# A written-out order, a rearranged start, and additions by GpSimd's DMAs in a two-layer attention and MLP kernel

## The chip, the cores and the metric

The kernel runs on one core of a Trainium2 chip. The core has TensorE (PE, matmuls; its weight loads are shown as PEld), VectorE (DVE), ScalarE (ACT), GpSimd (POOL) and SyncE (SP), each with its own in-order instruction stream, and 16 DMA engines. DMAs are issued here from SP's queue, four from ScalarE's, and after the change also from GpSimd's. The metric is the device time of one execution in microseconds (us).

## The reference

Input is `x`, 2048 tokens of 640 float32 values. Two layers, each an attention block and an MLP block, use the same weights:

```python
x = x + _A_ref(_layernorm(x, axis=-1), A_wqkv, A_wo)
x = x + _B_ref(_layernorm(x, axis=-1), B_w1, B_b1, B_w2, B_b2)
```

The attention has 32 heads of 20 values. Each token attends to 8 tokens: itself and those 2, 4, ... 14 places before it. The MLP has 1536 hidden values, a GELU and two biases.

## The kernel before, in words

**Units.** Because the window steps by 2, even and odd tokens never meet. Each parity is cut in two, which makes four units of 512 tokens per layer, n = 0 to 3 for the first layer and n = 4 to 7 for the second. A unit has four token tiles t of 128 partitions x 640 values. Attention works in four head groups g.

**Precision.** Matmuls are float16 with each operand split in a high and a low part: high x high, low x high and high x low are added in PSUM. So a product over 640 has 5 blocks x 3 passes = 15 matmuls. Weights are scaled by 64 (`WS`) before they are split, and results by 1/64.

**A unit's path.** Layernorm (`layernorm`); transposes of the normed high and low parts (for unit 0 on TensorE through `turn`, L498 to L506, and for all others by DMA transposes from SP, L623); the q, k, v product (`qkv`, L657, 480 columns per group and tile; ScalarE evicts it, L663); a spill to DRAM and a fetch back with neighbours; attention on VectorE (`attention`, L731 to L769: long multiplies and reductions, 2.8 to 5.5 us each); transposes by DMA (L789); the projection (`project`, two halves c of 320 columns per tile, L800); its addition to the token stream (L806, on VectorE, straight from PSUM); a second layernorm (its power of -1/2 is a small GpSimd instruction, L593; the normed tile is ScalarE's L613, its float16 cast L616); and the MLP (`mlp`, L837 to L879, and for the last three units `mlp_fast`, L1014 to L1133, a scheme with seven products instead of eight). The MLP's second bias `b2` is added to the token stream after the second layernorm has read it: by a GpSimd instruction (L627) in units 0 to 6, by VectorE in unit 7.

**Buffers.** The product and projection results share three PSUM tiles, "ps"; the MLP accumulates in "acc". Normed float32 tiles go through two SBUF tiles "y", transposed tiles through three "yT", MLP weight tiles (320 KB, `c<-mw`) through three buffers for each of two sets.

**Order.** The kernel writes its own schedule. Every operation is entered in a plan with a duration, a priority and what it needs; `Plan.run` simulates the engines and yields the order in which instructions are emitted, and so the order of each engine's stream. `NUDGE` shifts some priorities. GpSimd's long elementwise work (`laid`) is put beside VectorE's reductions, with a dependency on the VectorE instruction in front.

**The start.** SP loads two token tiles, the three weight parts of head group 0 (q, k, v columns, 400 KB each), then the other two token tiles and the other groups' weights. ScalarE makes the high parts of the weights and VectorE the low ones (L443, L444). 72 small matmuls of an identity (L1143) fill TensorE until the first product; their place among the other TensorE work comes from the plan.

Of the kernel before, what the change touches and what calls it, by code (L numbers as in the profile page):

```python
# [10 lines left out]
AF = mybir.ActivationFunctionType  # L11
# [36 lines left out]

SPARE = (0.5, 2.0)
# [21 lines left out]
NUDGE = {  # L71
# [8 lines left out]
    ('qkvp', 3, 3, 2): 31.2, ('qkvp', 3, 3, 3): 7.9, ('wop', 3, 3, 0): -748.4, ('qkvp', 4, 2, 0): -50.2, ('at', 18): 4.2, ('ad', 18, 0, 4): 266.2,  # L80
# [8 lines left out]
    ('sr', 3, 1): 292.5, ('out', 0, 3, 1): 52.4, ('hp', 4): 646.6, ('outh', 0, 0, 3): 31.8, ('out', 0, 3, 3): 2.5, ('outh', 0, 5, 2): 104.4,  # L89
    ('outh', 0, 5, 3): 92.5, ('out', 0, 6, 2): 3.3, ('hp', 19): 8.3, ('outh', 0, 8, 3): 2.2, ('outh', 1, 4, 1): 2.1, ('out', 1, 11, 3): -176.9,  # L90
    ('out', 2, 11, 1): 12.2, ('outh', 3, 0, 0): 234.1, ('outh', 3, 3, 3): 379.3, ('outh', 3, 9, 3): 417.2, ('xr', 3, 0): -142.9, ('x', 1, 3, 0): -137.5,
    ('x', 1, 3, 1): -154.6, ('hlo', 64): 75.8, ('outh', 4, 6, 2): 30.3, ('out', 4, 8, 1): 3.5, ('out', 4, 8, 3): 0.6, ('hp', 69): 1.4, ('hp', 70): 0.7,
# [7 lines left out]
class Plan:  # L100
# [27 lines left out]
    def add(self, eng, dur, prio, emit, need=(), give=(), use=(), table=None, move=0.0, lazy=False, spare=0.0,  # L128
            opens=0, beside=0, until=None):
        prio += NUDGE.get(give[0], 0.0)  # L130
        o = dict(eng=eng, dur=dur, prio=prio, emit=emit, need=need, give=give, use=use, table=table,
                 move=move, lazy=lazy, spare=spare, opens=opens, beside=beside, until=until, behind=None, ins=None, n=len(self.ops))
        self.ops.append(o)
        for u in use:
            if u not in self.users and u[0] in self.ORDERED and u not in self.line.setdefault(u[0], []):
                self.line[u[0]].append(u)
            self.users[u] = self.users.get(u, 0) + 1

    def run(self):
        when = {}  # L140
        waiting = {}
        ready = {}
        left = {}
        for o in self.ops:
            left[o["n"]] = len(set(o["need"]))
            for k in set(o["need"]):
                waiting.setdefault(k, []).append(o)
            if not left[o["n"]]:
                ready.setdefault(o["eng"], []).append(o)
        clock = {e: 0.0 for e in self.LAG}  # L150
        table = None
        bus = hw = 0.0
        order = []
        windows = []
        shut = sum(o["opens"] > 0 for o in self.ops)
        ahead = None

        def window(o, t):
            for w in windows:
                if o["beside"] > w[3]:  # L160
                    continue
                s = max(t, w[0])
                if s + o["dur"] <= w[1] + self.OVER:
                    return s, w
            return None, None

        def start(o):
            t = clock[o["eng"]]
            if o["move"]:
                t = max(t, hw, bus - self.AHEAD * o["lazy"] - 99 * (not o["lazy"]))  # L170
            for k in o["need"]:
                e, w, spare = when[k]
                w = w + (self.LAG[e] if e != o["eng"] else 0.06 * (e != "pe")) + spare * (o["eng"] == "pe")
                t = max(t, w)
            new = {}
            for u in o["use"]:
                if u in self.slot:
# [1047 lines left out]
```

## Time and profile before

| | |
|---|---|
| median of 3 runs | 1146.87 us (1146.6 to 1147.41) |
| profiled execution | 1146.79 us, of which the span from first to last instruction is 1145.0 |
| TensorE busy | 1136.1 us (99% of the span) |
| VectorE busy | 1068.0 us (93%) |
| ScalarE busy | 565.1 us (49%) |
| GpSimd busy | 138.5 us (12%) |
| SP's DMA queue | 254.55 MB, 75.9% of the 16 DMA engines' time |

In rows of groups, the numbers after the bar are total busy us and mean ns of one instruction, then the idle time of that engine just before them and what ended it. In rows of waits: total us, times, longest. In the chain: start us, us, what. In rows of DMAs: count, KB of one, median us from issue to landing. In rows of stretches: busy us of PE, PEld, DVE, ACT and POOL with instruction counts, granted TensorE clock, DMA share, GB/s.

### The profile page before, as it was taken

What the parts mean: (1) busy time and instruction counts of PE and PEld (TensorE: products, weight loads), DVE (VectorE), ACT (ScalarE), POOL (GpSimd) and SP (SyncE); (2) the same over time, 40 slices, a digit from 0 to 9 for tenths busy, and PEclk for the clock granted to TensorE, in tenths of its full rate; (3) what the DMA queues carried; (4) which work ended last, traced back from release to release, by engine and by line L of the source; (5) the groups of instructions that cost most, each with busy time, mean ns of one, the idle gap of its engine ahead of it and who ended that gap; (6) DMA issues with size and microseconds to landing.
All of it is one profiled execution on the core that took longest, in us unless ns stands there. A gap on an engine that the chain in (4) does not pass through costs nothing.

```text
span 1145.0 us, 17774 instructions
## 1 busy us (share of the span) xinstructions
PE 1136.1 (99%) x6952; PEld 648.3 (57%) x6952; DVE 1068.0 (93%) x1007; ACT 565.1 (49%) x985; POOL 138.5 (12%) x98
## 2 busy tenths in 40 slices
PE   8999999999999999999999999999999999999998
PEld 5444446577654565446555554556455546556886
DVE  7999999999999999999999999999989999988482
ACT  6476444446474438433645462355538452367360
POOL 1001000111110112100212021111320110200000
PEclk9999999999999999999999999999999999999999
DMA  9998999988976566856665946567578966788745
GB/s 289 300 331 262 294 364 276 256 280 277 251 208 187 192 203 159 223 182 172 191 191 177 224 149 184 189 195 186 147 235 276 298 227 200 228 202 219 232 138 173
DMA packets 256400, 256.73 MB, mean 224 GB/s; under 512 B 135916, under 2 KB 206908, under 8 KB 256316
## 3 DMA queue, kind: packets, MB, share of 16 engines
q1 hardware_dynamic: 252092, 254.55, 75.9%
q10 hardware_dynamic: 4224, 1.05, 0.5%
q8 instruction: 54, 0.88, 0.3%
q14 instruction: 30, 0.25, 0.1%
HBM read 175.64 MB, written 48.71 MB: 196 GB/s over the span
## 4 chain that ended last, share of the span: by engine, by line
PE 95%; DVE 3%; DMA 1%; SPq 1%; ACT 0%; issue 0%; POOL 0%; ACTq 0%; DVEq 0%
PE ps L657 34%; PE ps L837 17%; PE acc L856 13%; PE ps L800 10%; PE acc L1114 9%; PE ps L1051 5%; PE acc L859 3%; PE acc L1014 3%; DVE pr L757 1%; DVE pr L765 1%; DMA c<-mw 1%; PE ps L1014 1%; DMA pr<-in_A_wqkv_dram 0%; SPq L789 0%; DMA wq<-in_B_w_dram 0%; PE acc L498 0%
## 5 line engine op out<-in xcount | busy, mean ns | idle before, releaser
L657 PE MATMUL ps<-wq,yT 128*128 128x480 f16 x1920 | 390.6, 366 | 0.0
L657 PEld LDWEIGHTS <-yT 128*128 128x128 f16 x1920 | 187.7, 98 | 199.9
L837 PE MATMUL ps<-yT,c 128*128 128x512 f16 (+1 forms) x1080 | 204.2, 344 | 0.0
L856 PE MATMUL acc<-c,act 128*128 128x512 f16 x720 | 199.8, 379 | 0.0
L731 DVE TENSOR_TENSOR pr<-qk 128x2560 f32<-128x2560 f32 (+1 forms) x44 | 176.9, 4025 | 0.8 <-DMA qk<-spill 0.6
L757 DVE TENSOR_TENSOR pr<-sm,v 128x2560 f32<-128x2560 f32 (+1 forms) x44 | 176.9, 4031 | 0.3
L735 DVE TENSOR_REDUCE sm<-pr 128x128 f32<-128x2560 f32 (+1 forms) x44 | 176.5, 4014 | 0.0
L837 PEld LDWEIGHTS <-c 128*128 128x128 f16 x1080 | 103.5, 98 | 86.3
L663 ACT ACTIVATE ev<-ps 128x480 f32<-128x480 f32 x128 | 72.2, 568 | 160.5 <-PE ps L657 146.6
L859 PE MATMUL acc<-c,act 128*128 128x128 f16 x720 | 148.2, 219 | 0.0
L765 DVE TENSOR_TENSOR pr<-pr 128x2560 f32<-128x2560 f32 (+2 forms) x88 | 141.2, 1617 | 0.1
L800 PE MATMUL ps<-wo,yT 128*128 128x320 f16 x960 | 132.4, 299 | 0.5 <-DVE xf L806 0.5
L856 PEld LDWEIGHTS <-act 128*128 128x128 f16 x720 | 70.2, 98 | 81.4
L800 PEld LDWEIGHTS <-yT 128*128 128x128 f16 x960 | 93.7, 98 | 38.0 <-issue 0.6
L843 ACT ACTIVATE act<-ps,b 128x512 f32<-128x512 f32 (+1 forms) x72 | 44.3, 615 | 132.7 <-PE ps L837 126.8
L778 POOL TENSOR_TENSOR ohl<-o,ohl 128x640 f16<-128x640 f32 x24 | 43.4, 1809 | 420.2 <-DVE sm L748 71.0
L1114 PE MATMUL acc<-c,wq 128*128 128x320 f16 x630 | 93.1, 299 | 0.0
L593 POOL TENSOR_TENSOR ln<-ln,half 128x2 f32<-128x2 f32 (+1 forms) x30 | 45.8, 1526 | 376.4 <-ACT ln L590 376.4
L1051 PE MATMUL ps<-yT,c 128*128 128x512 f16 x360 | 78.8, 379 | 0.5 <-DMA c<-mw 0.3
L1114 PEld LDWEIGHTS <-wq 128*128 128x128 f16 x630 | 61.6, 98 | 24.5 <-issue 0.2
L859 PEld LDWEIGHTS <-act 128*128 128x128 f16 x720 | 68.3, 98 | 5.8
L576 ACT ACTIVATE junk<-xf 128x640 f16<-128x640 f32 x56 | 41.1, 733 | 59.8 <-DVE xf L806 48.7
(136 smaller groups left out, 1120.1 us busy)
## 6 DMA issues: line engine op xcount, KB each, us to landing
c<-mw SPq DMA_DIRECT2D x180, 320.0 KB, 3.7
spill<-ev SPq DMA_DIRECT2D x64, 480.0 KB, 3.9
qk<-spill SPq DMA_DIRECT2D x32, 880.0 KB, 6.5
v<-spill SPq DMA_DIRECT2D x32, 880.0 KB, 5.7
c<-msp SPq DMA_DIRECT2D x36, 320.0 KB, 3.5
qk<-spill SPq DMA_DIRECT2D x32, 320.0 KB, 3.4
c<-mw SPq DMA_DIRECT2D x54, 160.0 KB, 2.9
mw<-c SPq DMA_DIRECT2D x24, 320.0 KB, 5.3
```

Source lines behind the costliest of these rows:

```text
L657: nc.tensor.matmul(ps, transposed(yk)[:, a * KD + k, t * P:(t + 1) * P], wq[:, b, k, g], start=j == 0, stop=j == 3 * KD - 1)
L663: act(3 * GC, -400 + n, lambda i=i, pk=pk, ek=ek: nc.scalar.activation(tile_of(*ek)[:, :, i], tile_of(*pk)[:, :3 * GC].rearrange("p (a c) ...
L731: return nc.vector.tensor_mul(pr(pk), w[:, HALO + m + t0:HALO + m + t0 + TH, None, :].to_broadcast([P, TH, W, GC]), windows(w, t0, [GC, W] ...
L735: dve(E, G - 0.7, lambda pk=pk, t0=t0: nc.vector.tensor_reduce(lg(t0, t0 + TH).rearrange("p t w h -> p (t w h)"), pr(pk).rearrange("p t w ...
L757: return nc.vector.tensor_mul(pr(vk).rearrange("p t w (h d) -> p t (w h) d", d=DH), lg(t0, t0 + TH).rearrange("p t w h -> p t (w h)")[:, : ...
L765: dve(TH * w * GC, G - 0.9, lambda vk=vk, w=w: nc.vector.tensor_add(pr(vk)[:, :, 0:w], pr(vk)[:, :, 0:w], pr(vk)[:, :, w:2 * w]), need=[la ...
L800: nc.tensor.matmul(tile_of(*pk)[:, :D // 2], transposed(yk)[:, a * KD + k, t * P:(t + 1) * P], wo[:, b, k, c * D // 2:(c + 1) * D // 2], s ...
L837: nc.tensor.matmul(tile_of(*pk)[:, :nt], tile_of(*ck)[:, a, k * P:(k + 1) * P], transposed(yk)[:, c * KD + k, t0 * P:t1 * P], start=i == 0 ...
L856: nc.tensor.matmul(acc[i], w, tile_of(*wk)[:, c, :BANK], start=e == 0 and (a, c) == PASS[0], stop=end, skip_group_check=True)
L859: nc.tensor.matmul(acc[4][:, i * P:(i + 1) * P], w, tile_of(*wk)[:, c, BANK:], start=e == 0 and i == t0 and (a, c) == PASS[0], stop=end, s ...
L1051: nc.tensor.matmul(tile_of(*pk), tile_of(*ck)[:, a, k * P:(k + 1) * P], transposed(yk)[:, c * KD + k, :], start=i == 0, stop=i == 3 * KD - 1)
L1114: nc.tensor.matmul(acc[bank][:, :HD], tile_of(*hk)[half][:, a, slot, t * P:(t + 1) * P], load()[:, z, c], start=q in FIRST and i == 0 and ...
```

## The change

**The order.** The planner, `NUDGE` and the simulation go. In their place stand three lists: `ORDER`, the numbers of all 3549 operations (counted as the code enters them) in the order of emission; `PLACES`, the buffer that each tile takes; and `BESIDE`, for GpSimd's elementwise work, the VectorE operation in front. Read against the count, the streams begin so:

- SP: token tiles 0, 1, 2; weight parts (group 0, part 0), (0, 2); token tile 3; (0, 1); (1, 1), (3, 2), (1, 2), (3, 1), (1, 0); transpose of tile 2; (2, 0), (2, 1); a tile of unit 1; two clears; another tile of unit 1; transpose of tile 3; ...
- ScalarE: cast of tile 0; high weights (0, 0), (0, 2); casts of tiles 1, 2; transposed copy of tile 0 high; high weights (0, 1); transposed copies of tile 0 low, tile 1 high, tile 1 low; high weights (1, 1), (1, 2); ...
- VectorE: statistics of tiles 0, 1; norm 0; statistics of tile 2; low of tile 0; norms 1, 2; low weights (0, 0); low of tiles 1, 2; low weights (0, 2), (0, 1); ...
- TensorE: 24 small matmuls, tile 0 high's transposes, 16 small, tile 0 low's, 24 small, tile 1 high's, 8 small, tile 1 low's; then the q, k, v products: tile 0 of group 0 high x high and low x high, tile 1 of group 0, tile 0's high x low, tile 2 of group 0, tile 0 of group 1, tile 3 of group 0, ...

In unit n = 3 TensorE's stream around the projection is, with (t, c) for its products and single MLP passes between: (0, 0), (0, 1), (3, 0), four passes, (1, 1), (1, 0), seven passes, (3, 1), one group of passes, (2, 0). GpSimd's additions come in the order of tiles 0, 1, 3, 2 there.

**The start.** Unit 0's tiles 2 and 3 are transposed by DMA instead of on TensorE. For tiles 0 and 1 the copy of the transposed low part moves from VectorE to ScalarE. The first product (tile 0, group 0) is split in three of five matmuls: high x high needs only high parts.

**The additions.** In units n = 2 to 6 ScalarE evicts the projection's halves to a "y" tile, scaled, and one DMA from GpSimd's queue per token tile adds it to the token stream in SBUF (`accum_op`). In units 2 to 7 the bias is added by such a DMA too. Units 0 and 1 (and 7 for the projection) keep the old instructions.

```diff
+ADDED = (2, 3, 4, 5, 6)
...
+    def adding(kb, prio, emit, need=(), give=(), use=()):
+        plan.add("pool", 1.0, prio, emit, need, give, use, move=1.0 * kb / 330.0, land=1.0)
...
     def run(self):
...
+        places = iter(PLACES.replace("\n", ""))
         for o in self.ops:
...
             for u in o["use"]:
                 if u not in self.slot:
...
+                    self.slot[u] = int(next(places))
+            o["behind"] = self.ops[BESIDE[o["n"]]] if o["n"] in BESIDE else None
+        return [self.ops[int(n)] for n in ORDER.split()]
...
-                if a:
+                if a and t not in (0, 1):
                     return nc.vector.tensor_copy(to, ps)
                 else:
                     nc.scalar.activation(to, ps, AF.Copy)
...
-            if n == 0 and not twice:
+            if n == 0 and not twice and t not in (2, 3):
                 turn(first(t), t, name, hk, yk)
                 continue
...
-                last = lambda by, t=t: by.tensor_tensor(x[u][:, t], x[u][:, t], b2, op=OP.add)
-                if n == N - 1:
...
+                if n in (2, 3, 4, 5, 6, 7):
+                    adding(P * D * 4 / 1e3, -200 + n, lambda t=t: nc.gpsimd.dma_start(x[u][:, t], b2, accum_op=OP.add),
+                           need=[("y", name, t), "b2"], give=[("xb", n, t)])
...
+                if n == 0 and g == 0 and t == 0:
+                    def part(a, b, t=t, g=g, pk=pk):
+                        for k in range(KD):
+                            nc.tensor.matmul(tile_of(*pk)[:, :3 * GC], transposed(yk)[:, a * KD + k, t * P:(t + 1) * P], wq[:, b, k, g],
+                                             start=(a, b, k) == (0, 0, 0), stop=(a, b, k) == (0, 1, KD - 1))
+
+                    last = []
+                    for a, c in ((0, 0), (1, 0), (0, 1)):
+                        here = [("yT", ("a", n), t, a)] + [(("wq", "wqh")[1 - c], g, i) for i in range(3)]
+                        mm(KD * 3 * GC, 5, -500, lambda a=a, c=c, part=part: part(a, c), need=here + last,
+                           give=[("qkvp", n, t, g) if c else ("qkvq", a)], use=[pk, yk])
+                        last = [("qkvq", a)]
...
-                dve(D // 2, -700 + n, residual, need=[("wop", n, t, c)], give=[("xh", n, t, c)], use=[pk])
+                if n in ADDED:
+                    act(D // 2, -700 + n, lambda c=c, pk=pk, rk=rk: nc.scalar.activation(
+                        tile_of(*rk)[:, c * D // 2:(c + 1) * D // 2], tile_of(*pk)[:, :D // 2], AF.Copy, scale=1.0 / WS),
+                        need=[("wop", n, t, c)], give=[("we", n, t, c)], use=[pk, rk])
+                else:
+                    dve(D // 2, -700 + n, residual, need=[("wop", n, t, c)], give=[("xh", n, t, c)], use=[pk])
+            if n in ADDED:
+                adding(P * D * 4 / 1e3, -700 + n, lambda t=t, rk=rk: nc.gpsimd.dma_start(x[u][:, t], tile_of(*rk), accum_op=OP.add),
+                       need=[("we", n, t, c) for c in range(2)], give=[("xh", n, t, 0), ("xh", n, t, 1)], use=[rk])
```

More of the change, by code (lines that the diff above doesn't have):

```diff
@@ L139, in run @@
     def run(self):
[L140 to L143, printed above, removed]
+        places = iter(PLACES.replace("\n", ""))
         for o in self.ops:
[L145 to L177, printed above, removed]
-                    t = max(t, self.since[u])
-                else:
-                    fs = self.free[u[0]]
-                    if u[0] in self.ORDERED and self.line[u[0]][self.turn.get(u[0], 0)] != u:
-                        return None
-                    i = new.get(u[0], 0)
-                    if i >= len(fs):
-                        return None
-                    t = max(t, sorted(fs)[i][0])
-                    new[u[0]] = i + 1
-            if o["beside"] and (shut or windows):
-                s, _ = window(o, t)
-                return s if s is not None or shut and not o["until"](ready, when) else t
-            return t
@@ L229, in run @@
             for u in o["use"]:
                 if u not in self.slot:
-                    fs = self.free[u[0]]
-                    fs.sort()
-                    self.turn[u[0]] = self.turn.get(u[0], 0) + 1
-                    self.since[u], self.slot[u] = fs.pop(0)
-            if o["move"]:
-                clock[e] = t + o["dur"]
-                hw = t + o["dur"]
-                s = max(t + o["dur"] + self.REACH, bus)
-                bus = s + o["move"]
-                end = bus + self.LAND
-            else:
-                clock[e] = end = t + d
@@ L243, in run @@
-            o["at"] = t
-            order.append(o)
-            for u in o["use"]:
-                self.users[u] -= 1
-                self.last[u] = max(self.last.get(u, 0.0), end + self.LAG[e] * (u[0] != "pr" or e != "dve"))
-                if not self.users[u]:
-                    self.free[u[0]].append((self.last[u], self.slot[u]))
-            for k in o["give"]:
-                when[k] = (e, end, o["spare"])
-                for w in waiting.pop(k, ()):
-                    left[w["n"]] -= 1
-                    if not left[w["n"]]:
-                        ready.setdefault(w["eng"], []).append(w)
@@ L256, in run @@
-        order.sort(key=lambda o: o["at"])
-        self.time = max(clock.values())
-        self.order = order
-        return order
+                    self.slot[u] = int(next(places))
+            o["behind"] = self.ops[BESIDE[o["n"]]] if o["n"] in BESIDE else None
+        return [self.ops[int(n)] for n in ORDER.split()]
 def v_cost(n):
@@ L509, in turn @@
                use=[hk, pk])
-            (dve if a else act)(D, prio - 1, copy, need=[("turn", name, t, a)], give=[("yT", name, t, a)], use=[pk, yk])
+            (dve if a and t not in (0, 1) else act)(D, prio - 1, copy, need=[("turn", name, t, a)], give=[("yT", name, t, a)], use=[pk, yk])
     def at(b, t):
@@ L558, in layernorm, with quick @@
         fast = not twice and n < FAST
+        SLOW = ()
+        def quick(t):
+            return fast and (n, t) not in SLOW
         def first(t):
             return prio if n or twice else -1100 if t == 0 else -900 + t
-        for t in range(m if fast else 0):
+        for t in filter(quick, range(m)):
             def stats(t=t):
@@ L574, in layernorm @@
             pool(0.5, prio, rstd, need=[("sq", name, t), "half"], give=[("r", name, t)], use=[lk])
-        for t in range(0 if fast else m):
+        for t in (t for t in range(m) if not quick(t)):
             act(D, prio, lambda t=t: nc.scalar.activation(junk, x[u][:, t], AF.Copy, scale=-1.0 / D,
@@ L587, in layernorm @@
         cut = CUTS[n > 0][twice]
-        for t0 in range(0, 0 if fast else m, cut):
+        for t0 in range(0, m, cut):
             t1 = min(m, t0 + cut)
+            if quick(t0):
+                continue
             act(cut, prio - 1, lambda t0=t0, t1=t1: nc.scalar.activation(
```

75 lines of the change are left out of this document (25 added, 50 removed), and 136 rows, old and new, of tables (BESIDE, NUDGE, ORDER).

## The prediction

> **What bounds the kernel now.** I read the busy shares first, then what TensorE waited for, then the chain that ended last, then the first 25 us instruction by instruction.
>
> ```profile
> span 1145.0 us, 17774 instructions
> PE 1136.1 (99%) x6952; PEld 648.3 (57%) x6952; DVE 1068.0 (93%) x1007; ACT 565.1 (49%) x985; POOL 138.5 (12%) x98
> PE 95%; DVE 3%; DMA 1%; SPq 1%; ACT 0%; issue 0%; POOL 0%; ACTq 0%; DVEq 0%
> ```
>
> TensorE is busy for 99% of the span and 95% of the chain is TensorE. VectorE at 93% looks like a second bound, but what counts is whether TensorE ever waits for it:
>
> ```profile
> PE acc L498 <- ACT hl L616: 2.8, 1, 2.8
> PE acc L1143 <- POOL ident L415: 1.3, 1, 1.3
> PE ps L800 <- DVE xf L806: 0.5, 1, 0.5
> PE acc L498 <- DVE hl L618: 0.4, 2, 0.2
> PE ps L1051 <- DMA c<-mw: 0.3, 1, 0.3
> PE ps L1051 <- ACT act L1057: 0.2, 1, 0.2
> ```
>
> The L498 and L1143 waits lie in the start. After it TensorE waited three times, 0.5 + 0.3 + 0.2 = 1.0 us in all. The chain in order of time gives the pace and both ends:
>
> ```profile
> 23.96 160.99 PE ps L657 x795
> ...
> 323.31 21.26 PE ps L657 x105
> ...
> 438.56 0.73 PE acc L859 x13
> 439.29 2.59 PE acc L856 x12
> ...
> 530.94 16.30 PE ps L800 x120
> ...
> 1141.75 0.49 DVE xf L1133
> ```
>
> One L657 matmul (480 columns) takes 160.99 / 795 = 0.2025 us, a group of 15 takes 3.04, a projection product of 15 (L800) 16.30 / 8 = 2.04, and one pass of the MLP's second product 2.59 / 12 + 0.73 / 13 = 0.27. From 23.96 to 1141.75 TensorE has work without a break but for the 1.0 us. What can be won is therefore in the start, in that 1.0 us, and nowhere else; what can be lost is unlimited.
>
> ```profile
> 7.29 0.87 ACT L443 ACTIVATE wq<-pr 128x800 f16<-128x800 f32 x1 [5.29 <-DMA pr<-in_A_wqkv_dram]
> ...
> 9.87 0.87 ACT L443 ACTIVATE wq<-pr 128x800 f16<-128x800 f32 x1 [0.32 <-DMA pr<-in_A_wqkv_dram]
> ...
> 12.23 3.20 PE L657 MATMUL ps<-wq,yT 128*128 128x480 f16 x15
> ...
> 17.17 6.24 PE L657 MATMUL ps<-wq,yT 128*128 128x480 f16 x30
> ...
> 23.24 0.72 PE L498 MATMUL acc<-ident,hl 128*128 128x128 f16 x10
> ```
>
> When the last transposes on TensorE (L498) end at 23.96, 45 L657 matmuls are done. Had they run without a break up to there, they would have begun at 23.96 - 45 x 0.2025 = 14.85. I call this the effective start; the change is worth whatever it moves it, plus or minus waits later.
>
> **The start, part by part.** The rows of the operations that move, and of the transfers:
>
> ```profile
> L616 ACT ACTIVATE hl<-y 128x640 f16<-128x640 f32 x60 | 43.0, 728 | 11.1 <-DMA yT<-hl 6.8 <-DVE y L609 4.2
> L443 ACT ACTIVATE wq<-pr 128x800 f16<-128x800 f32 x6 | 5.0, 859 | 5.6 <-DMA pr<-in_A_wqkv_dram 5.6
> L506 ACT ACTIVATE yT<-acc 128x640 f16<-128x640 f16 x4 | 2.8, 692 | 0.0
> ...
> xf<-in_A_x_dram SPq DMA_DIRECT2D x16, 320.0 KB, 5.3
> pr<-in_A_wqkv_dram SPq DMA_DIRECT2D x6, 400.0 KB, 7.1
> ```
>
> Loads land in order. With two token tiles ahead, the first weight part had landed by 7.29 (1040 KB); the third by 9.87 (1840 KB): 800 KB in 2.58 us, 310 KB per us. The new queue order is three token tiles, parts 0 and 2, the fourth tile, then part 1. So part 2 lands with 1760 KB at 7.29 + 720 / 310 = 9.6 and part 1 with 2480 KB at 9.87 + 640 / 310 = 11.9, 2 us later than before. ScalarE then has, in its new order from 9.6 on: part 2 (0.86), two casts of normed tiles (2 x 0.73), tile 0's high transposed copy (0.69) and part 1 (0.86): 13.5. Then TensorE can begin high x high, 1.3 us later than the 12.23 of before.
>
> But it then stops less. Splitting the first group in three lets it start without the low halves: two fives until 15.5, while ScalarE makes the other three copies (3 x 0.69, so 15.6; the two moved there from VectorE are in this). Tile 1's fifteen run 15.6 to 18.6, the last five to 19.6. That is 30 matmuls, an effective start of 19.6 - 6.1 = 13.5.
>
> Tiles 2 and 3 lose their 20 TensorE transposes and get DMA transposes instead. Tile 2's is thirteenth on SP's queue, with 4480 KB ahead, which land at 9.87 + 2640 / 310 = 18.4. Its own 320 KB take at least 1.0 us more, 19.4; at most the whole unloaded time below, 3.3, so 21.7. I take 20.1, nearer the first because the request has long been issued: 0.5 us late. Tile 3's is needed after two more groups, at 26.2; 1545 KB and itself follow tile 2, 19.4 + 6.0 = 25.4, in time. Effective start 14.0, a gain of 0.85 us. These are the transposes' rows, of the whole run and of the loaded queue at 30 to 70 us:
>
> ```profile
> DMA to landing us min/median/max: 3.3/5.0/9.5
> ...
> L623 SPq DMA_TRANSPOSE yT<-hl x4: 3058/3820/4522, 37.6 to 54.2; - x4
> ...
> DMA to landing us min/median/max: 7.7/8.6/9.5
> ```
>
> **The additions by DMA.** In units n = 2 to 6 the projection's 40 VectorE additions from PSUM go; 40 ScalarE evictions and 20 accumulating DMAs take their place. In n = 2 to 7 the bias is added by 24 such DMAs instead of 20 GpSimd and 4 VectorE instructions.
>
> ```profile
> L806 DVE SCALAR_TENSOR_TENSOR xf<-ps,xf 128x320 f32<-128x320 f32 x64 | 29.9, 485 | 7.4 <-PE ps L800 6.8
> L627 DVE TENSOR_TENSOR xf<-xf,b 128x640 f32<-128x640 f32 x4 | 3.3, 816 | 0.0
> L663 ACT ACTIVATE ev<-ps 128x480 f32<-128x480 f32 x128 | 72.2, 568 | 160.5 <-PE ps L657 146.6 <-issue 5.6 <-DMA act<-in_B_w_dram 4.9
> c<-mw SPq DMA_DIRECT2D x180, 320.0 KB, 3.7
> out_dram<-xf SPq DMA_DIRECT2D x4, 320.0 KB, 3.5
> L593 POOL TENSOR_TENSOR ln<-ln,half x30: 548/802/6501, 70.3 to 1032.9; 128x2 f32<-128x2 f32 x26, 128x1 f32<-128x1 f32 x4
> 420.00:900.00 480.00, 479.52 (x2805) 256.11 (x2803) 468.55 (x338) 244.73 (x432) 80.52 (x46) 1.00 0.67 194
> ```
>
> VectorE saves 40 x 0.485 + 4 x 0.816 = 22.7 us. I cost this at nothing, as TensorE waited 0.5 us for VectorE after the start; it is at most part of that 1.0 us. ScalarE gains 40 x 0.45 = 18 us (0.45 is below the 0.57 that 480 columns take); it is idle for half of 420 to 900. The DMA engines get 44 x 320 KB in about 700 us, 5% more, at a share of 0.67; weight tiles have three buffers, and without that cover a late one costs about a microsecond.
>
> The price that matters is the delay from a tile's second eviction to the landing of its addition, D. No row shows an accumulating DMA or one issued by GpSimd. From below it is 3.5, a plain 320 KB transfer; from above 3.7 + 6.5 = 10.2, if the issue on GpSimd is held as long as its slowest power (L593). I take 3.7 + 320 / 310 = 4.7, for the second read that an addition needs: SP's transfers are the nearest rows in size and route, the power is another kind of work.
>
> Whether D shows depends on what stands behind it. The evicted tile sits in one of two "y" buffers until the DMA has landed; the next tile's eviction in that buffer waits on ScalarE, in order, with every eviction behind it, while TensorE has three PSUM buffers. In n = 3 the written order gives TensorE, between tile 0's second product and the product that needs the waiting buffer, three products and eleven passes: 3 x 2.04 + 11 x 0.27 = 9.1 us. Less two evictions of 0.45 and handovers, D may be 8. The same reading for n = 4, 5 and 6 gives 7.5 to 8; the layernorm's reads have more room (in n = 2 the MLP starts 28 us after the last product). At 4.7 nothing shows: 0 us.
>
> The Trainium skill (DMA: Bandwidth & Descriptors, "Anatomy of one DMA — SWDGE (gpsimd) path") gives such a DMA 2.0 us plus its bytes over 436 GB/s, by estimate 2.8 us here. No run here shows it; by it the sum stays as it is.
>
> **The sum.** 1146.79 (profiled execution: span 1145.0 and 1.79 around it; the median of the runs is 0.08 higher) - 0.85 + 0 = 1145.9.
>
> **The rivals.** *Late additions (slower).* GpSimd's issue is held up by VectorE. For it: the power that took 6.5 us instead of 0.55, about one long VectorE instruction more, at 93% VectorE. Against: the median power took 0.8. It decides once D passes 8, and costs the excess once per unit: D of 9.5, as the slowest transpose, gives 5 x 1.5 = 7.5, so 1146.79 - 0.85 + 7.5 = 1153.4; at 10.2, 11 us and 1156.9. The Trainium skill (SBUF — State Buffer, "Who interferes with whom") lets two-input VectorE work block GpSimd's reads but, by inference, not its writing of descriptors; by that rule this rival falls, and the slow power fits its first half.
>
> *Late transposes.* As at 37 us: 8.6 from issue to landing, SP held 3.8 each. Tile 2 issued near 12.9, an estimate from VectorE's new order, lands at 21.5, 1.9 late; tile 3 issued about 20 lands at 28.6, 1.0 late. Effective start 13.5 + 2.9 = 16.4, 1.55 worse: 1148.3. Against it: at 12.9, 4480 - 1840 - 3.0 x 310 = 1710 KB stand in front, which at 310 KB per us are 5.5 us and not 7.6.
>
> *All on time (faster).* Both transposes in time (13.5) and no wait after the start: 1146.79 - 1.35 - 1.0 = 1144.4. Against it: the 1.0 us has three different causes.
>
> *VectorE's relief is worth nothing*: the change does not do what less VectorE work suggests. That is inside my forecast.
>
> **How the numbers follow.** Forecast 45%, late transposes 15%, late additions 22%, all on time 18%. This kernel's measurement tells 0.2%, 2.3 us, from no change: faster is below 1144.6, slower above 1149.2. Faster: the last case, 0.18. Slower: late additions, with a little of late transposes, 0.25. The rest, 0.57, is no change. The range runs from 1143.7, a little under the best case, to 1152.0, D near 9; my forecast's own is 1144.8 to 1147.5.
>
> **What would show it.** Right: TensorE's first L657 row near 13.5 with five matmuls; its wait for a transposed tile before the third group under 1 us; no L498 row after 14; GpSimd's DMAs landing in 4 to 6 us; ScalarE never waiting for them with TensorE waiting behind; VectorE near 1045 us busy and the end hardly moved. Wrong: landings over 8 us with "ps" waits of TensorE on ScalarE in units n = 2 to 6, or new waits spread over the whole written-out order, which I priced at nothing beyond the old 1.0.

## The result and the profile after

The kernel became slower: 1167.1 us median against 1147.22, ratio 1.0172 (95% interval 1.0150 to 1.0193). I had forecast 1145.9 with a range to 1152.0. The profiled execution took 1163.56 us, the fastest of five; lines of its page:

```profile
span 1161.6 us, 17680 instructions
PE 1136.2 (98%) x6932; PEld 646.4 (56%) x6932; DVE 1065.8 (92%) x959; ACT 573.7 (49%) x1023; POOL 178.5 (15%) x122
...
q0 software_dynamic: 6336, 14.42, 7.1%
...
PE 71%; DVE 10%; issue 9%; DMA 6%; POOL 2%; ACT 2%; SPq 1%; DVEq 0%; ACTq 0%; POOLq 0%
```

TensorE does the same work in the same 1136 us, but 71% of the chain is TensorE where it was 95%. GpSimd's queue moves 14.42 MB and takes 7.1% of the DMA engines' time. The start, from the chain in order of time:

```profile
13.38 2.03 PE ps L670 x10
15.41 3.04 PE ps L663 x15
18.45 1.01 PE ps L670 x5
19.46 164.03 PE ps L663 x810
183.49 16.30 PE ps L820 x120
```

The last five of the split first group end at 19.46 after 30 matmuls: effective start 19.46 - 30 x 0.2025 = 13.4, and no wait for tile 2's transpose in this execution. The first projection begins at 183.49. Before it was

```profile
184.95 16.30 PE ps L800 x120
```

so 1.46 us had been won up to there. The rest was lost behind it. TensorE's longest waits after the change, without the two of the start (3.8 and 1.4 us):

```profile
...
PE acc L1142 <- DMA c<-msp: 3.4, 2, 2.2
PE ps L1079 <- ACT wq L1096: 3.2, 1, 3.2
PE ps L865 <- ACT y L831: 2.1, 2, 1.1
PE acc L887 <- DVE act L876: 2.0, 1, 2.0
...
PE ps L663 <- ACT y L831: 1.3, 1, 1.3
PE ps L1079 <- DMA c<-mw: 1.2, 1, 1.2
PE ps L820 <- ACT y L831: 1.2, 1, 1.2
PE ps L663 <- ACT ev L682: 0.9, 1, 0.9
```

Three kinds stand there: weight tiles that come late (`c<-mw`, `c<-msp`, and behind the `c<-mw` one of 1.2 us ScalarE's cast of the hidden values that were computed with it, L1096), projection evictions (L831, 2.1 + 1.3 + 1.2 = 4.6 us), and VectorE's L876 (a two-input instruction of the MLP). The additions, bias (L632) and projection (L837), by their source lines:

```profile
L632 POOL DMA_DIRECT2D xf<-b x24: 862/916/1545, 509.1 to 1056.3; - x24
DMA to landing us min/median/max: 3.6/7.1/10.4
...
L837 POOL DMA_DIRECT2D xf<-y x20: 862/874/1045, 421.5 to 883.5; - x20
DMA to landing us min/median/max: 3.6/5.8/8.7
```

The issue itself takes about 0.9 us in the median and 1.55 at most, so no long VectorE instruction (up to 5.5 us) shows in it; landing takes 5.8 to 7.1 us in the median.

### The profile page after: what moved, and what is told of

Same layout as the page of the kernel before. It is cut to its first block, busy times and chain, and to the rows that moved or that the text cites. A ratio compares the mean times of both kernels' runs of the same rounds, so it can differ in the third digit from the quotient of the medians.

```text
span 1161.6 us, 17680 instructions
## 1 busy us (share of the span) xinstructions
PE 1136.2 (98%) x6932; PEld 646.4 (56%) x6932; DVE 1065.8 (92%) x959; ACT 573.7 (49%) x1023; POOL 178.5 (15%) x122
## 3 DMA queue, kind: packets, MB, share of 16 engines
q0 software_dynamic: 6336, 14.42, 7.1%
q10 hardware_dynamic: 4224, 1.05, 0.6%
## 4 chain that ended last, share of the span: by engine, by line
PE 71%; DVE 10%; issue 9%; DMA 6%; POOL 2%; ACT 2%; SPq 1%; DVEq 0%; ACTq 0%; POOLq 0%
PE ps L663 25%; PE ps L865 11%; PE acc L884 9%; PE acc L1142 7%; PE ps L820 7%; PE ps L1079 6%; DMA xf<-y 3%; PE acc L1042 3%; PE acc L887 2%; DVE pr L776 2%; DVE pr L750 2%; DVE sm L754 2%; POOL xf L637 1%; DVE pr L784 1%; POOL ohl L797 1%
## 5 line engine op out<-in xcount | busy, mean ns | idle before, releaser
L884 PE MATMUL acc<-c,act 128*128 128x512 f16 x720 | 204.4, 379 | 0.7 <-DVE act L876 0.7
L865 PEld LDWEIGHTS <-c 128*128 128x128 f16 x1080 | 103.5, 98 | 89.6 <-issue 2.5
L820 PE MATMUL ps<-wo,yT 128*128 128x320 f16 x960 | 135.3, 299 | 1.2 <-ACT y L831 1.2
L597 POOL TENSOR_TENSOR ln<-ln,half 128x2 f32<-128x2 f32 (+1 forms) x30 | 49.8, 1661 | 339.6 <-ACT ln L594 339.6
L797 POOL TENSOR_TENSOR ohl<-o,ohl 128x640 f16<-128x640 f32 x24 | 60.2, 2508 | 269.2 <-ACT ohl L795 187.4
L1079 PEld LDWEIGHTS <-c 128*128 128x128 f16 x360 | 35.0, 98 | 46.7 <-DMA c<-mw 5.4
(139 smaller groups left out, 1153.4 us busy)
```

Of the source, the lines that this page charges most:

```text
L797: low = lambda by: by.tensor_tensor(tile_of(*hk)[:, :, 1, g * GC:(g + 1) * GC], tile_of(*ok), hi(), op=OP.subtract)
L820: nc.tensor.matmul(tile_of(*pk)[:, :D // 2], transposed(yk)[:, a * KD + k, t * P:(t + 1) * P], wo[:, b, k, c * D // 2:(c + 1) * D // 2], s ...
L865: nc.tensor.matmul(tile_of(*pk)[:, :nt], tile_of(*ck)[:, a, k * P:(k + 1) * P], transposed(yk)[:, c * KD + k, t0 * P:t1 * P], start=i == 0 ...
L884: nc.tensor.matmul(acc[i], w, tile_of(*wk)[:, c, :BANK], start=e == 0 and (a, c) == PASS[0], stop=end, skip_group_check=True)
L1079: nc.tensor.matmul(tile_of(*pk), tile_of(*ck)[:, a, k * P:(k + 1) * P], transposed(yk)[:, c * KD + k, :], start=i == 0, stop=i == 3 * KD - 1)
```

## The experiments

The runs were made in groups, each group on one chip together with the kernel before, whose median was 1146.9 to 1147.4 in every group. The groups ran on several chips.

**Leaving out one thing at a time.** The start alone:

```diff
-ADDED = (2, 3, 4, 5, 6)
+ADDED = ()
-                if n in (2, 3, 4, 5, 6, 7):
+                if n in ():
 # ORDER: the changed start up to tile 2 of group 1, then the order of the kernel before
```

> One part alone. The new start (order of loads, split first group, DMA transposes for tiles 2 and 3) with the order, the additions and the pairs of the kernel before behind it. My working of the start: the changed kernel's projection of unit 0 began at 183.49 us against 184.95, so if the start's gain is kept in an otherwise old order, 1147.2 - 1.4 = 1145.8 us (1145.3 to 1146.5). The theory that the loss of 20 us lies in the start's knock-on effects (every later transfer and buffer shifted): 1155 us or more. The theory that the start gains nothing by itself: 1147.2.

Measured: 1147.86 us, ratio 1.0003 (0.9994 to 1.0013). My 1145.8 did not come: no gain can be told, and no loss either. In its profiled execution tile 2's transpose was 0.6 us late (I had forecast 0.5) and the first projection began 0.5 us earlier than before, not 1.46.

```diff
-            if n in ADDED:
-                adding(P * D * 4 / 1e3, -700 + n, lambda t=t, rk=rk: nc.gpsimd.dma_start(x[u][:, t], tile_of(*rk), accum_op=OP.add),
```

> The changed kernel without the 20 DMAs that add the projection to the token stream (the evictions by ScalarE stay, and the sum is left out). Late projection additions (landings of 5.8 us median hold the two y buffers and with them ScalarE and TensorE): the time falls from 1167 to 1145 to 1150 us, and ScalarE's waits for a DMA on the y tile (21.0 us) go to 0. Misfit of the written order, or GpSimd's arithmetic stretched by VectorE: it stays at 1160 or above.

Measured: 1164.9 us, ratio 1.0150 (1.0112 to 1.0187). My first theory, late projection additions, fell: without them nearly all of the loss is still there.

```diff
-adding(... nc.gpsimd.dma_start(x[u][:, t], tile_of(*rk), accum_op=OP.add) ...)
-adding(... nc.gpsimd.dma_start(x[u][:, t], b2, accum_op=OP.add) ...)
```

> The changed kernel without any of the 44 accumulating DMAs (neither the projection nor, in units 2 to 7, the bias is added). It leaves the written order, GpSimd's arithmetic and the pairs as they are. Late additions of either sort: 1145 to 1148 us, 2 to 5 us below the run without projection additions if the bias additions cost something through the DMA engines. Misfit of the written order or of the pairs: 1158 us or above, as in the run without the projection additions.

Measured (both sorts of additions left out, evictions kept): 1149.87 us, 1.0022 (1.0013 to 1.0032). So it is the bias additions that cost most, to which I had given no price of their own.

```diff
-BESIDE = {278: 298, 302: 649, 326: 163, 395: 403, 400: 538, ...
+BESIDE = {302: 649, 326: 340, 395: 403, 400: 2054, 410: 724, ...
```

> The changed kernel with the table that holds a GpSimd subtraction or addition back until a named VectorE operation is done written anew: 14 of 30 now start together with a one-input sum of VectorE (as every one did in the kernel before), the other 16 start as soon as their input is there; the waits of 16 bias DMAs for a VectorE operation are gone. Theory that stale pairs cost the time (GpSimd's subtraction mean 2508 ns against 1809, one addition 9671): 1155 us or less, and that mean back under 2.0 us. Theory of late additions: 1163 to 1168 us as the changed kernel.

Measured: 1162.8 us, 1.0140 (1.0113 to 1.0166); the interval overlaps that of the changed kernel. (By the lists it is 20 bias DMAs, not 16, that lose their wait for a VectorE operation here.) Read against the lists, each of the 49 GpSimd operations paired in the kernel before was followed on VectorE by the long one-input sum of attention; in the changed order 6 of 26 paired subtractions and additions are, as `BESIDE` kept the old partners while VectorE's order moved. The changed kernel's GpSimd addition:

```profile
L637 POOL TENSOR_TENSOR xf<-xf,b x8: 1535/1546/9671, 251.5 to 424.1; 128x640 f32<-128x640 f32 x8
```

One took 9.67 us instead of 1.55. The Trainium skill (SBUF — State Buffer, "Who interferes with whom") says that a VectorE instruction with two SBUF inputs contends with a GpSimd instruction that reads SBUF; the trace agrees: from 251.5 to 259.8 us, while this addition ran, VectorE issued nothing but two-input instructions. VectorE pays as well: in the changed kernel its one-input sum keeps its mean while a two-input product gets longer,

```profile
L754 DVE TENSOR_REDUCE sm<-pr 128x128 f32<-128x2560 f32 (+1 forms) x44 | 176.8, 4020 | 0.1
...
L763 DVE TENSOR_TENSOR sm<-sm 128x256 f32<-128x256 f32 x32 | 16.2, 506 | 0.2
```

where the kernel before has

```profile
L735 DVE TENSOR_REDUCE sm<-pr 128x128 f32<-128x2560 f32 (+1 forms) x44 | 176.5, 4014 | 0.0
...
L744 DVE TENSOR_TENSOR sm<-sm 128x256 f32<-128x256 f32 x32 | 13.2, 413 | 0.1
```

**The bias additions.** Left out alone; cut to 8 columns; alone in the old order; and the pairs again, without any addition:

```diff
-adding(... nc.gpsimd.dma_start(x[u][:, t], b2, accum_op=OP.add) ...)
```

> The changed kernel without the 24 DMAs that add the bias in units 2 to 7 (that bias is left out); the projection's 20 additions stay. Leaving out both sorts gave 1149.9 us, leaving out the projection's alone 1164.9. If the two prices add up, the bias additions cost 15 and the projection's about 2: 1152 us (1150 to 1154). If the loss needs either sort (both fill the same gap in the transfers): 1160 or above.

Measured: 1155.85 us, 1.0077 (1.0062 to 1.0092): 6 us above the run without any, so the prices do not add up; the projection's 2 us beside the bias are 6 without it.

```diff
-nc.gpsimd.dma_start(x[u][:, t], b2, accum_op=OP.add)
+nc.gpsimd.dma_start(x[u][:, t, :8], b2[:, :8], accum_op=OP.add)
```

> The changed kernel with each of the 24 bias DMAs cut from 640 columns to 8 (the rest of the bias is left out in units 2 to 7): the same 24 issues at the same places of GpSimd's queue with the same waits, a hundredth of 320 KB to move. Theory that the bias additions' traffic delays the loads beside it (the DMA share in 850 to 960 us is 0.98 to 1.04 with them against 0.81 to 0.89 without): it falls to what leaving them out gives, 1150 to 1154 us. Theory that their waits in GpSimd's queue hold back the powers and subtractions behind them: it stays at 1163 to 1168.

Measured: 1157.71 us, 1.0099 (1.0080 to 1.0119). With all issues and waits in place but no bytes, about 9.4 of the 20 us are gone: what costs is the transfer, not the place in GpSimd's queue.

Much of it is lost late in the kernel, as 13 of the 24 are issued from 850 us on. The stretches from 850 to 960 us in the kernel before, in the changed kernel and with 8 columns, in this order:

```profile
850.00:900.00 50.00, 49.52 (x318) 28.53 (x316) 45.81 (x56) 35.93 (x55) 1.80 (x2) 1.00 0.93 278
900.00:960.00 60.00, 60.00 (x340) 31.65 (x339) 59.03 (x65) 27.05 (x33) 7.45 (x5) 1.00 0.77 231
```

```profile
850.00:900.00 50.00, 47.83 (x306) 27.51 (x304) 45.61 (x38) 31.76 (x53) 7.60 (x9) 1.00 1.04 280
900.00:960.00 60.00, 55.56 (x294) 26.38 (x293) 55.83 (x60) 31.39 (x41) 6.83 (x7) 1.00 0.98 277
```

```profile
850.00:900.00 50.00, 50.00 (x319) 28.70 (x318) 48.82 (x41) 34.01 (x56) 8.09 (x9) 1.00 1.03 282
900.00:960.00 60.00, 60.00 (x335) 30.70 (x334) 57.35 (x68) 33.89 (x44) 9.93 (x7) 1.00 0.83 243
```

TensorE is idle for 6.6 us there in the changed kernel and not at all with 8 columns; the two profiled executions are 7.2 us apart. It waits there for projection evictions (1.2 and 1.0 us), for a weight tile (1.2) and for ScalarE's cast behind that tile (3.2).

```diff
-ADDED = (2, 3, 4, 5, 6)
+ADDED = ()
 # ORDER as with the start alone; the bias DMAs of units 2 to 7 as in the change
```

> The written order of the kernel before with the new start, and one part of the additions: the bias of units 2 to 7 is added by DMAs, issued at the places where GpSimd (unit 7: VectorE) did the sum before; the projection stays with VectorE. The same with GpSimd's sums gave 1147.9 us. Theory of traffic, whatever the order: several us more, 1152 to 1163, with TensorE's waits on weight tiles after 850 us. Theory that the new order alone is at fault: 1147 to 1149.

Measured: 1169.82 us, 1.0193 (1.0165 to 1.0222): 22 us for 24 DMAs in an order that is otherwise the old one (and without the wait for a VectorE operation that 20 of them have in the changed kernel). The new order is not what makes them dear. In its profiled execution TensorE waits 9.1 us for weight tiles (`c<-mw`), 6.3 at the longest.

```diff
 # neither addition; BESIDE written anew
-BESIDE = {278: 298, 302: 649, 326: 163, ...
+BESIDE = {302: 649, 326: 340, ...
```

> The changed kernel without any of the 44 accumulating DMAs, as in the run that gave 1149.9 us, and with the pairs of GpSimd and VectorE written anew for this order (14 paired with a one-input sum, the rest free). In that run TensorE waited 2.0 us for VectorE at 270 us, behind a GpSimd addition that took 9.7 us instead of 1.5. Theory of stale pairs: that wait goes, 1147 to 1148 us. If the pairs cost nothing: 1149.9.

Measured: 1146.19 us, 0.9996 (0.9986 to 1.0006), 3.7 us below the same kernel with stale pairs, with intervals apart. In the stretch from 200 to 300 us TensorE's busy time with the stale pairs and with the new ones (columns as in the table of stretches):

```profile
200.00:300.00 100.00, 97.58 (x707) 64.51 (x705) 95.57 (x93) 50.81 (x100) 20.30 (x8) 0.98 0.85 272
```

```profile
200.00:300.00 100.00, 99.77 (x739) 66.86 (x738) 98.57 (x94) 51.80 (x102) 22.57 (x9) 1.00 0.90 282
```

**What about their traffic is dear.**

```diff
-nc.gpsimd.dma_start(x[u][:, t], b2, accum_op=OP.add)
+nc.gpsimd.dma_start(x[u][:, t], b2)
```

> The changed kernel with its 24 bias DMAs made plain copies: the same source, target, size, place and waits, but the target is overwritten instead of added to (so from unit 2 on the token stream is lost; the work's amount is the same). Theory that it is the addition in the DMA which is dear (24 additions took 33 us of engine time each by the queue's share, where SP's transfers of that size take some 18): it falls most of the way to the narrow DMAs' 1157.7, to 1158 to 1161 us, and the queue's share of engine time by about a quarter. Theory that any 320 KB on these engines at these places costs it: it stays at 1163 to 1168.

Measured: 1158.93 us, 1.0100 (1.0065 to 1.0134). As copies they cost 8.2 us less and take 5.1% of the engines' time with the projection's, not 7.1. That is little over the narrow ones, but the runs spread from 1154.8 to 1165.4.

```diff
-ADDED = (2, 3, 4, 5, 6)
+ADDED = ()
-                if n in (2, 3, 4, 5, 6, 7):
+                if n in (2, 3, 4):
```

> The old order with the new start as in the run that gave 1169.8 us with DMAs for the bias of units 2 to 7 and 1147.9 with none, now with DMAs in units 2 to 4 alone (12 of 24, all before 850 us, where the DMA share is near 0.65). Theory that the additions hurt where the transfers have no room (after 850 us, share 0.8 to 0.9): 1147.5 to 1150 us. Theory that each costs the same: half of 22, 1159 us.

Measured: 1156.84 us, 1.0075 (1.0046 to 1.0103). Half of the DMAs cost 9 of the 22 us although they lie where the engines have room on average: in this order my theory that only the full stages are dear fell. This run's trace, of the slowest of its four executions (1151.8 to 1159.2), shows one place. From 442 us two bias additions are in flight beside the transposes of the same layernorm:

```profile
442.00:464.00 22.00, 16.88 (x83) 8.02 (x82) 10.18 (x9) 8.12 (x16) 2.39 (x3) 0.98 1.24 115
464.00:472.00 8.00, 6.15 (x21) 2.59 (x21) 7.40 (x6) 7.97 (x21) 2.46 (x2) 0.63 0.85 242
```

The same stretch with the start alone:

```profile
442.00:464.00 22.00, 22.00 (x111) 10.60 (x109) 21.97 (x18) 20.31 (x44) 6.02 (x4) 1.00 0.96 228
464.00:472.00 8.00, 8.00 (x39) 3.69 (x38) 8.00 (x8) 6.04 (x9) 0.00 (x0) 1.00 1.07 224
```

The DMA engines are busy throughout in both, but with the additions they move 115 GB/s instead of 228. The transposes on SP from 430 to 470 us, with the additions and then without:

```profile
DMA to landing us min/median/max: 4.3/14.7/21.2
```

```profile
DMA to landing us min/median/max: 4.3/6.5/8.7
```

One of 21.2 us holds VectorE and ScalarE, and TensorE in the end:

```profile
PE ps L658 <- ACT ev L677: 7.0, 1, 7.0
```

TensorE idles from about 459 to 466 us, and its granted clock is 0.63 over the 8 us from 464: cut finer, 0.50 from 464 to 468 and 1.00 again from 470. By estimate the 4 us of work at half speed lose 2 us more. The Trainium skill (TensorE: Matmul & The Clock Gate, "Part 1: The HAM clock gate (the "warmup" mystery)") says that the clock halves after an idle window of some 3.4 us; the row agrees. So do a wait of 5.2 us in a run below (0.50 from 928 to 932 us) and the one of 3.2 us in the changed kernel, after which the clock stayed at 1.00.

```diff
-nc.gpsimd.dma_start(x[u][:, t], tile_of(*rk), accum_op=OP.add)
+nc.gpsimd.dma_start(x[u][:, t, :8], tile_of(*rk)[:, :8], accum_op=OP.add)
```

> The changed kernel without the bias DMAs, as in the run that gave 1155.9 us, and with the projection's 20 DMAs cut from 640 columns to 8 (the rest of the projection's result is left out). Without either it was 1149.9, so the projection's DMAs cost 6. Theory of traffic: 1150 to 1151.5 us. Theory of landing time (the two y buffers wait for a landing that is 4 us even for 4 KB, as the narrow bias DMAs showed): 1153 to 1156, with ScalarE still waiting at the eviction for the DMA.

Measured: 1152.27 us, 1.0042 (1.0029 to 1.0055), between the two theories. 3.6 of the projection's 6 us go with their bytes; the other 2.4 are not certain, as the interval touches that without any addition.

```diff
-                if n in (2, 3, 4, 5, 6, 7):
+                if n in ():
 # BESIDE written anew
```

> A whole kernel: the changed one with the bias of units 2 to 7 added by GpSimd and VectorE again, as before the change, and the pairs written anew for this order; the projection's result is still added by DMAs. If the parts add up: 1149.9 without any addition, less 3.7 for the pairs, and 6 for the projection's DMAs give 1152 us (1149 to 1156, as the 20 sums on GpSimd are new in this order). If the projection's additions cost nothing once bias traffic and stale pairs are gone: 1146 to 1148.

Measured: 1152.16 us, 1.0040 (1.0025 to 1.0055), as the sum of the parts said: the projection's DMAs alone make this order slower than the kernel before.

**Both alone on the chip.** Groups of DMAs, with no other work but VectorE's clearing between them:

```diff
 for i in range(2):
     nc.gpsimd.dma_start(add[i], src, accum_op=OP.add)
 for i in range(4):
     nc.sync.dma_start_transpose(low[i], hl)
```

> Not the model at all: seven groups of DMAs, four times over, each group apart from the next, with nothing else on the chip's engines. Four DMA transposes (320 KB each) alone; two accumulating DMAs of GpSimd (320 KB) alone; both together; two plain copies of GpSimd with the transposes; two copies alone; four loads of 320 KB alone; two accumulating DMAs with the loads; two accumulating DMAs of 8 columns with the transposes. Theory that an accumulating DMA and a DMA transpose block each other: together the transposes land in 11 us or more (in the runs with bias DMAs the slowest took 11 to 21 us, in all others at most 8.8), while the copies leave them within 2 us of their own time and the loads lose 2 us at most. Theory of plain traffic: the additions lengthen transposes and loads alike, by the 2 us that each one's bytes take, and copies as much as additions.

Measured, by source line: transposes alone (L53), additions alone (L56), both together (L59, L61), copies with transposes (L64, L66), copies alone (L69):

```profile
L53 SPq DMA_TRANSPOSE low<-hl x16: 1253/1459/1601, 24.3 to 460.4; - x16
DMA to landing us min/median/max: 3.4/3.5/3.8
...
L56 POOL DMA_DIRECT2D add<-src x8: 851/1066/1217, 43.2 to 475.2; - x8
DMA to landing us min/median/max: 3.6/4.3/4.9
...
L61 SPq DMA_TRANSPOSE low<-hl x16: 1465/1899/3797, 60.9 to 499.9; - x16
DMA to landing us min/median/max: 3.5/5.3/7.2
...
L66 SPq DMA_TRANSPOSE low<-hl x16: 1301/1464/3314, 83.6 to 520.8; - x16
DMA to landing us min/median/max: 3.5/4.5/4.9
...
L69 POOL DMA_DIRECT2D add<-src x8: 536/537/545, 104.0 to 536.2; - x8
DMA to landing us min/median/max: 2.4/2.7/2.9
```

An addition of 320 KB lands in 4.3 us where a copy takes 2.7, and its issue costs 1.07 us instead of 0.54. The Trainium skill's fit (DMA: Bandwidth & Descriptors, "Anatomy of one DMA — SWDGE (gpsimd) path") gives 2.8 by estimate: the copy agrees, the addition does not. But together they only share the time, 7.2 at most: the theory that the two block each other for 11 us or more fell here. The group with loads says nothing, as its loads were issued 8 us before the additions.

```diff
 # the old order with the start and 24 bias DMAs; each behind a later VectorE operation
+BESIDE: 831: 974, 836: 975, 841: 976, 846: 978, 1027: 2534, 1032: 1175, ...
```

> The old order with the new start and all 24 bias DMAs, which gave 1169.8 us, with one difference: each DMA is held back (behind a named VectorE operation) to a stretch in which by the order no DMA transpose runs within some 6 us, one after another. Same bytes, same number. Theory that the additions collide with the transposes that the same layernorm issues right beside them: 1147 to 1151 us and no transpose over 9 us. Theory of traffic as such: 1160 or above. A few us of it may come back as GpSimd's queue waits for the held DMAs.

Measured: 1155.36 us, 1.0067 (1.0046 to 1.0087): 14 of the 22 us are back with the same 24 additions, only apart from the transposes and from each other (the run doesn't tell these two apart). That lies between the two theories. What stays is above all one wait of 5.2 us for a weight tile at 925 us, between additions issued at 922 and 929.

```diff
+nc.sync.dma_start(qk[i], far)
+nc.sync.dma_start(spill[i], ev)
+nc.vector.tensor_tensor(big[2], big[0], big[1], op=OP.add)
```

> Not the model: groups of DMAs apart from each other, four times over. In the run before, two accumulating DMAs and four transposes alone on the chip only shared the time (transposes 5.3 us median against 3.5 alone, 7.2 the slowest), so that pair does not explain the 21 us in the model. Here each group has four transposes; with and without two accumulating DMAs beside them: with VectorE's two-input sums running; with two transfers of 480 KB to HBM; with two loads of 880 KB from HBM; with all of these and two loads of 320 KB; and all of these with plain copies in place of the additions. Theory that VectorE's work makes them crawl: slowest transpose over 10 us in the group with sums and additions, under 8 without sums. Theory that a third kind of transfer does it: over 10 us in the group with that transfer and additions, and at least 3 us less in the same group without the additions and with the copies. Theory that only bytes count: each group takes the sum of its parts' own times (two additions 3.5 us, four transposes 6).

Measured: nothing over 9.2 us. With additions the slowest transpose took 7.8 us beside VectorE's sums, 7.8 with the transfers of 480 KB, 7.4 with the loads of 880 KB, and 9.0 with all (5.3 without the additions, 6.6 with copies). Neither VectorE nor a third kind of transfer makes them crawl for 20 us. The loads of 880 KB had been issued some 9 us before the additions and landed in at most 6, so that the groups with them say little of these loads.

**Copies at the dear places.**

```diff
-nc.gpsimd.dma_start(x[u][:, t], b2, accum_op=OP.add)
+nc.gpsimd.dma_start(x[u][:, t], b2)
```

> The old order with the new start and the 12 bias DMAs of units 2 to 4 made plain copies: same places, same bytes, the target overwritten (so the token stream is lost from there on). With additions it was 1156.8 us and one transpose took 21 us. Theory that the addition in the DMA makes it crawl beside transposes: 1148 to 1151 us, transposes at most 9 us. Theory that it is bytes beside the transposes: 1155 to 1158.

Measured: 1149.57 us, 1.0021 (1.0007 to 1.0035): 7.3 of the 9 us are gone. The stretch that crawled, in a profiled execution that is one of the fastest of six:

```profile
442.00:464.00 22.00, 22.00 (x111) 10.59 (x109) 20.33 (x17) 18.38 (x41) 3.04 (x3) 1.00 0.98 230
```

The slowest transpose there took 10.9 us, more than the 9 that I allowed. The same edit with all 24:

> The same with all 24 bias DMAs of units 2 to 7 made plain copies; with additions 1169.8 us, with none 1147.9. Theory of the addition: 1149 to 1156 us. Theory of bytes: 1165 or above.

Measured: 1157.94 us, 1.0081 (1.0056 to 1.0107), 2 us above what I expected: 12 of 22 us are gone, 10 stay, and one transpose still took 14.6 us. So the adding is a good half of the price in this run (12 of 22) and more in the two others (7.3 of 9 with 12 DMAs, 8.2 of 11 in the changed kernel). The rest is the bytes, with late weight tiles and late transposes again.

## Why the prediction was wrong

**The start** was right in its mechanism and small in its size: first product at 13.4 (forecast 13.5), effective start 13.4 (14.0), tile 2's transpose late by nothing in one profile and by 0.6 in another (0.5). That it cannot be told from no change, the run with the start alone shows.

**The step that failed** is the sentence "The DMA engines get 44 x 320 KB in about 700 us, 5% more, at a share of 0.67", with "a late one costs about a microsecond" behind it: it left the bias additions at a price of nothing. Three things in it were wrong. An addition is not a plain transfer of its size: the bytes are 14.42 of 271.8 MB, 5%, but the queue takes 7.1 points of the engines' time. The share of 0.67 is a mean from 420 to 900 us; 13 of the 24 bias additions come from 850 us on, where the kernel before had 0.93 and 0.77 and the changed kernel has 1.04 and 0.98 (the rows above). And the bias additions got no delay and no rival of their own: all the care went to the projection's D. They cost 9 to 11 us in this order (1167.1 against 1157.7 with 8 columns and 1155.9 without), 15 without the projection's additions (1164.9 against 1149.9) and 22 in the old order. For the microsecond of a late tile I had no row; the one at 940 us cost 1.2 + 3.2 us.

The 21-us transpose is shown in the old order only. In the changed kernel unit 2's bias additions are issued from 509 to 573 us, when the transposes of their layernorm (449 to 459 us, at most 4.6 us to land) are long done. Three additions at 573 us do run beside unit 3's transposes; one of these took 10.6 us, and no wait of TensorE follows up to 655 us.

**D** was mis-sized, and so was its threshold. I took 4.7 and let nothing show below 7.5 to 8. The median from issue to landing is 5.8 (4.8 without the bias additions), the slowest 8.7; the 0.3 to 0.4 us from eviction to issue, which D holds too, come on top. These steps stand on the changed kernel's chain:

```profile
543.34 6.58 DMA xf<-y
...
665.86 8.42 DMA xf<-y
...
678.07 6.05 POOL ohl L797
684.12 7.71 DMA xf<-y
...
875.09 7.27 DMA xf<-y
```

Two of the four landings lie below 7.5. The one at 684.12 had a D of 15: its eviction ended at 676.8, but GpSimd's subtraction (L797) stood before it in the queue and took 6.1 us, beside a two-input product of VectorE, instead of 1.4. My sign of being wrong came: TensorE waited 4.6 us for these evictions. The projection's additions cost 6 us when nothing else is added. The room that I read off the written order holds only if TensorE and VectorE are where the order has them; I did not test it against an order that is already late.

**The written order**, "which I priced at nothing beyond the old 1.0", cost 3.7 us through its pairs. Both lists stood in the diff, and to see it I would have had to look up which VectorE operation follows each partner in the new order. With fresh pairs and neither sum done at all it takes 1146.2, near my 1145.9; that is luck, as the start's 0.85 us cannot be told in the run with the start alone. VectorE's relief came out as 2.2 us of busy time, not 22.7: the instructions went as said, but stretched two-input rows, as L763 above, take most of it back.

**The rivals.** Late additions came nearest in size (1153.4 to 1156.9), for the most part by the wrong mechanism: it had GpSimd's issue held up by VectorE, and the projection's issues take 0.86 to 1.05 us throughout. The Trainium skill's rule (SBUF — State Buffer, "Who interferes with whom"), that by inference two-input work does not block descriptor writing, agrees with that; I let it speak against the whole rival, though landings can be late by other ways, and the queue can be held by a slow GpSimd instruction, as at 678 us. Late transposes at the start did not come.

**The account.** Changed kernel 1167.1; the bias additions' bytes 9.4; their issues 1.9, within the spread; the projection's additions 6.0; the pairs 3.7; what is left is 1146.2. By the intervals each term is good to some 2 to 3 us. The order in which the parts are taken out matters, as the 2 and 6 us for the projection and the 11 and 15 for the bias show.

**Open** is why two additions and four transposes take 20 us together in the model and 12 alone on the chip (59.8 to 72.2 us in the first of the four rounds). VectorE's sums and 480 KB writes were tried and are not it. How often it happens is open too: it was seen in one execution. No whole kernel tried here beats the kernel before.

## What to carry to other kernels

Price an accumulating DMA by its time on the DMA engines and not by its bytes, and look at the share and at what else is issued at its own moment, not at a mean share: an addition that becomes possible together with a transpose can run beside it, as it did in the old order. When a written order is regenerated, every list that refers to neighbours in the old order has to be regenerated too. A long wait of TensorE (5.2 and 7.0 us here, not 3.2) is paid in part again in clock behind it.

## What the runs showed of the hardware

- An accumulating DMA of 320 KB within SBUF takes 4.3 us from issue to landing alone on the chip and 0.87 to 1.07 us of GpSimd's queue; a plain copy 2.7 and 0.54. In the model (the old order) the 24 bias additions took 4.3% of the engines' time, as copies 2.6%.
- Cut to 8 columns an addition still landed after 4.3 us in the model and after 3.0 beside transposes alone on the chip (medians): few bytes do not make it early.
- Beside transposes, additions halved what the busy DMA engines moved, 115 against 228 GB/s for 22 us in one execution; copies at the same place left it at 230.
- A GpSimd addition that met VectorE's two-input work took 9.67 us instead of 1.55, and a DMA behind such an instruction in GpSimd's queue is issued that much later.
- After waits of 5.2 and 7.0 us TensorE's granted clock was 0.50 for the next 4 us of its work or so; after one of 3.2 us it stayed at 1.00.
